# Attention with a mixture of experts: a new order of the first six slots, and nineteen fewer dummy matmuls

## The chip, the cores and the metric

The kernel runs on one core of a Trainium2 chip. The metric is the device time of one launch in microseconds (us). TensorE (PE) multiplies matrices, VectorE (DVE), ScalarE (ACT) and GpSimd (POOL) work on elements, and SyncE (SP) issues nearly all transfers.

## The reference

The first phase is causal attention over 8 batches of 8 heads, 576 positions of 64 features, with a bias that decays with the running sum of a learned scalar:

```python
scores = scale * np.matmul(q, k.transpose(0, 1, 3, 2))
s_pos = np.maximum(s, 0.0)
cum = np.cumsum(s_pos, axis=-1)
bias = -(cum[:, :, :, None] - cum[:, :, None, :])
scores = np.where(causal, -1000000000.0, scores + np.minimum(bias, 0.0))
scores = scores - np.max(scores, axis=-1, keepdims=True)
attn = np.exp(scores)
attn = attn / (np.sum(attn, axis=-1, keepdims=True) + 1e-09)
return np.matmul(attn, v).astype(np.float32)
```

The second phase takes its output as x (8 x 576 x 512). Each of 4 experts projects x to q, k and v of 64 features, does causal attention, and projects back by wo; each position sums the two experts that its gate logits rank highest, weighted by a softmax over the two.

## The kernel before

The work is cut into slots. A slot is a pair of heads of the first phase or a pair of experts of the second. For each slot there are: copies of the raw q and k to a high part in a short float format (L645 for q, L648 for k), subtractions that leave the low part (L688, L693), and a second copy of the raw q and k (L663, L666, L674, L679), so that a float32 product is made of a matmul with the low parts (L780, tiles `q_0` and `k_0` of the first kind) and one with the high parts, the bias rows and a row of minus the maxima (L786). Before the scores come approximate column maxima: bfloat16 matmuls (L714, tiles `mx`), a reduction on DVE (L728, `mcol`), a transpose (L749, `mt`), a copy on ACT (L753, `mr`), and a transfer of that row into the operand q (L758). Then ACT takes the exponential (L809), POOL masks and sums (L827 to L879), TensorE multiplies by v (L947) and ACT copies that out (L961, `pv`). Sums go by L895 or L997, a reciprocal (L1028), a row to DRAM and back (`rr`, `rb`, L1034 and L1039), and DVE scales (L1064). ACT and DVE then split x into a high part (L1068, `xh`) and a low part (L1072, `xl`), and TensorE projects (L1182, `pq`).

At the start the scalars s are loaded twice: for the first two slots in short pieces (`f_t`, L457), and for all (`s_t`, L492), scaled (L495), summed along rows (L496), completed by a matmul over the parts (L500), and split in three (L503 to L510); the result is written to DRAM (L1511, `cum`), from where later slots read their bias rows.

The order is by hand. Each instruction stands on its engine in the order in which the program calls the steps, and the steps are called as the table STEPS lists them: "n:x" is step x of slot n. In it m and M are the matmuls and the reduction of a bank of maxima, mt, mA and mq the transpose, copy and transfer of the row, s and E a bank of scores and its exponential, a the first matmuls of a bank of scores whose second part comes later, d masks and sums, e0 the last sum on POOL, b0 and B0 early sums of the rows on TensorE and their copy, h the high copies, l the low parts, lq and lk the second copies, hc the bias rows, p and P projections and their copies, ld, lv and w loads of heads, of v and of weights, cu to cx of slot -2 the running sums, cu of slot -1 the transfer of them to DRAM. A step named for slot n may belong to a slot ahead: what stands under slot -2 prepares slot 0. z is a dummy, a matmul of 128 columns (L1442) whose result nobody reads: five at the start and 48 in the table. Each is two passes on TensorE. Engines wait for each other by semaphores that follow from the operands; on each engine a later instruction never overtakes one that waits.

Of the kernel before, what the change touches and what calls it, by code (L numbers as in the profile page):

```python
# [13 lines left out]
OP = mybir.AluOpType  # L14
# [16 lines left out]
FIRST_IDLE, IDLE = 5, 48  # L31
# [49 lines left out]
def heads(t, at, c0, c1):  # L81
# [1482 lines left out]
```

## Time and profile before

| what | value |
|---|---|
| median of 3 runs | 636.24 us (635.65 to 637.52) |
| profiled execution | 635.62 us, its span 633.9 us |
| TensorE (PE) busy | 627.3 us, 99% of the span |
| VectorE (DVE) busy | 511.1 us, 81% |
| ScalarE (ACT) busy | 446.9 us, 70% |
| GpSimd (POOL) busy | 420.7 us, 66% |

The span runs from the first to the last instruction that the profiler recorded; the execution's time is 1.7 us longer. Busy time of TensorE holds the dummies too. Matmuls are pipelined, so a group's busy time is shorter than the sum of its durations.

### The profile page before, as it was taken

To read this page: it belongs to the slowest core of one execution; us is meant where nothing else is said; L and a number is where in the kernel's file an instruction comes from. 1 tells how busy PE (TensorE), PEld (TensorE's weight loads), DVE (VectorE), ACT (ScalarE), POOL (GpSimd) and SP (SyncE) were. 2 spreads that over 40 slices of the span, in tenths; PEclk is the share of its full clock that TensorE was granted. 3 is DMA by queue.
4 is the path that set the end of the run, shared out by engine and by line. 5 is a ranking of instruction groups with operands and counts; after the bars stand their busy time and mean duration, and the time that the engine had idled before them with its cause. 6 is when DMAs were issued, how large, how long until landed. Compare 5 with 4: busy or idle time off the path is not lost.

```text
span 633.9 us, 16442 instructions
## 1 busy us (share of the span) xinstructions
PE 627.3 (99%) x5912; PEld 533.8 (84%) x5912; DVE 511.1 (81%) x1447; ACT 446.9 (70%) x976; POOL 420.7 (66%) x527
## 2 busy tenths in 40 slices
PE   9999999999999999999999999999999999999997
PEld 7888988888888888788887898788888889788875
DVE  7989887976988978886889778798887978763784
ACT  8897678856786676775767766785676775576364
POOL 5665697768864976587667766588576676828030
PEclk9999999999999999999999999999999999999999
DMA  5555723553665267455725464672563543432404
GB/s 155 168 167 141 224 65 95 155 115 96 191 164 137 65 157 195 129 148 126 197 77 150 114 136 131 165 211 57 147 193 91 139 143 82 119 101 56 111 2 149
DMA packets 61966, 83.45 MB, mean 132 GB/s; under 512 B 27439, under 2 KB 36871, under 8 KB 61885
## 3 DMA queue, kind: packets, MB, share of 16 engines
q1 hardware_dynamic: 61741, 82.27, 48.0%
q8 instruction: 47, 0.77, 0.5%
q14 instruction: 34, 0.28, 0.1%
q10 hardware_dynamic: 144, 0.13, 0.1%
HBM read 44.60 MB, written 10.16 MB: 86 GB/s over the span
## 4 chain that ended last, share of the span: by engine, by line
PE 93%; ACT 3%; DVE 2%; DMA 1%; issue 0%; SPq 0%; ACTq 0%; DVEq 0%
PE pvp L947 20%; PE pq L1182 16%; PE s L780 12%; PE s L786 12%; PE mx L714 10%; PE pw L1182 7%; PE po L1182 7%; PE sm L997 4%; PE po L1151 1%; PE mt L749 1%; PE idle L1442 1%; DMA rb<-rr 1%; PE pw L1237 1%; PE pw L1242 1%; ACT k L648 1%; DVE unread L728 1%
## 5 line engine op out<-in xcount | busy, mean ns | idle before, releaser
L809 ACT ACTIVATE p<-s 128x512 f32<-128x512 f32 x288 | 159.1, 588 | 39.7 <-PE s L786 32.8
L728 DVE CUSTOM_DVE_ANT_0 unread<-mx,mask 128x256 uint8<-128x256 f32 (+6 forms) x384 | 142.2, 418 | 31.8 <-PE mx L714 30.5
L780 PE MATMUL s<-q,k 128*128 128x288 f32 (+5 forms) x672 | 166.9, 285 | 0.2 <-ACT p L809 0.2
L786 PE MATMUL s<-q,k 68*128 68x288 f32 (+5 forms) x672 | 159.9, 279 | 0.0
L827 POOL TENSOR_SCALAR_AFFINE_SELECT p<-p 128x256 f32<-128x256 f32 (+2 forms) x183 | 110.6, 606 | 71.7 <-ACT p L809 69.6
L780 PEld LDWEIGHTS s<-q,k 128*128 128x128 f32 (+1 forms) x672 | 122.3, 183 | 7.2 <-issue 2.2
L874 POOL TENSOR_TENSOR r<-r,p 128x640 f32<-128x640 f32 x84 | 120.4, 1433 | 6.8
L786 PEld LDWEIGHTS s<-q,k 68*128 68x128 f32 (+1 forms) x672 | 121.5, 182 | 1.1 <-DMA q<-mr 0.4
L688 DVE TENSOR_TENSOR q<-raw,q 64x576 fp32r<-64x576 f32 (+1 forms) x86 | 83.0, 974 | 21.6 <-ACT q L645 7.9
L947 PE MATMUL pvp<-p,v 128*64 128x64 f32 (+6 forms) x1024 | 99.6, 334 | 0.3 <-DVE mcol L728 0.3
L947 PEld LDWEIGHTS pvp<-p,v 128*64 128x64 f32 x1024 | 68.3, 136 | 23.7 <-ACT p L809 0.9
L693 DVE TENSOR_TENSOR k<-raw,k 64x576 fp32r<-64x576 f32 (+1 forms) x86 | 83.1, 976 | 5.3 <-DMA k<-k 3.3
L714 PE MATMUL mx<-k,q 67*64 67x320 bf16 (+7 forms) x960 | 81.6, 293 | 0.8 <-DVE mcol L728 0.6
L1182 PE MATMUL pq<-xh,wqkh 128*128 128x288 f32 x256 | 76.4, 299 | 0.0
L1182 PE MATMUL pq<-xl,wqkh 128*128 128x288 f32 x256 | 75.5, 295 | 0.0
L1182 PE MATMUL pq<-xh,wqkl 128*128 128x288 f32 x256 | 75.4, 295 | 0.0
L868 POOL TENSOR_TENSOR r<-p 128x128 f32<-128x128 f32 x37 | 22.3, 602 | 72.3 <-ACT p L809 72.3
L648 ACT ACTIVATE k<-raw 64x576 fp32r<-64x576 f32 x96 | 64.9, 680 | 3.1 <-DMA raw<-in_qk_dram 0.8
L714 PEld LDWEIGHTS <-q 67*64 67x64 bf16 x960 | 47.4, 109 | 22.2 <-issue 6.1
L645 ACT ACTIVATE q<-raw 64x576 fp32r<-64x576 f32 x96 | 64.9, 681 | 1.5 <-PE s L786 0.4
L961 ACT ACTIVATE pv<-pvp 128x256 f32<-128x256 f32 (+1 forms) x92 | 36.2, 402 | 36.5 <-PE pvp L947 35.7
L1200 ACT ACTIVATE raw<-pq 128x288 f32<-128x288 f32 x64 | 25.4, 404 | 35.2 <-PE pq L1182 35.2
(174 smaller groups left out, 1245.4 us busy)
## 6 DMA issues: line engine op xcount, KB each, us to landing
raw<-in_qk_dram SPq DMA_DIRECT2D x30, 576.0 KB
rb<-rr SPq DMA_DIRECT2D x92, 144.0 KB
q<-q SPq DMA_DIRECT2D x45, 288.0 KB
k<-k SPq DMA_DIRECT2D x39, 288.0 KB
v<-in_vm_dram SPq DMA_DIRECT2D x32, 256.0 KB
out_dram<-o SPq DMA_DIRECT2D x31, 256.0 KB
q<-mr SPq DMA_DIRECT2D x96, 2.2 KB
raw<-in_qk_dram SPq DMA_DIRECT2D x4, 288.0 KB
```

Source lines behind the costliest of these rows:

```text
L648: nc.scalar.activation(k2[0:64, j], get_raw(n, j)[64:128], AF.Copy)
L688: eng.tensor_tensor(a[64:128, j], get_raw(n, j)[0:64], q2[0:64, j].bitcast(F32), op=OP.subtract)
L693: eng.tensor_tensor(c[0:64, j], get_raw(n, j)[64:128], c[64:128, j].bitcast(F32), op=OP.subtract)
L714: nc.tensor.matmul(t[64 * j : 64 * j + 64, c0 : c0 + k1 - k0], q2[0:RC, 64 * qt : 64 * qt + 64], k2[0:RC, k0:k1], start=True, stop=True,)
L728: nc.vector.tensor_tensor_reduce(t[:, 0:w] if len(MBANKS[bi]) == 1 else unread[:, c0 and 448 : (c0 and 448) + w], t[:, c0 : c0 + w], mask[ ...
L780: nc.tensor.matmul(t[0:nk, c0 : c0 + q1 - q0], K1[r1(n)][:, j, k0 : k0 + nk], Q1[r1(n)][:, j, q0:q1], start=True, stop=False,)
L786: nc.tensor.matmul(t[0:nk, c0 : c0 + q1 - q0], K2[r2(n)][0 : RM + 1, j, k0 : k0 + nk], Q2[r2(n)][0 : RM + 1, j, q0:q1], start=False, stop= ...
L809: nc.scalar.activation(chunk_of(ci, 0, 512)[:, x % 2], tl[x], AF.Exp, scale=0.125)
L827: nc.gpsimd.affine_select(out=a, in_=a, pattern=[[0, a.shape[1]], [1, w]], compare_op=OP.is_ge, fill=0.0, base=0, channel_multiplier=-1,)
L874: add(r[:, :, q0:S], r[:, :, q0:S], chunk_of(2, c, c + S - q0), op=OP.add)
L947: nc.tensor.matmul(cur[h][64 * j : 64 * j + 64, q0 - PVC[h] : q1 - PVC[h]], vsl(j, kt), heads(ptile[n], at, c, c + q1 - q0)[:, j], start=f ...
L1182: nc.tensor.matmul(t[0:nk, 0:w], l, r, start=(x == 0), stop=(x == len(terms) - 1))
```

## The change

Nineteen dummies go: two ahead of the first complete score, and the seventeen that stood later, in the steps of slots 0 to 4. The scaling of the running sums moves from DVE to ACT, their last subtraction from DVE to POOL, the load of s behind the two loads of the first q and k, the transfer of the sums to DRAM behind the loads of v, and the second copy of slot 0's q on ACT is divided, the second head's part behind the copy of the maxima. Some 25 steps of slots 1 to 6 stand at other places in the table: high copies of slots 4 to 6, masks and sums of slots 1 to 4, maxima of slots 2 to 6, the early sums of slot 1, a bank of scores of slots 5 and 6, one load of heads, one of weights. Behind slot 6 the order is the same.

```diff
-FIRST_IDLE, IDLE = 5, 48
+FIRST_IDLE, IDLE = 5, 29
...
-    "-2:hc -2:cu -2:ld -2:h1 -2:h0 -2:z0 -2:z1 -2:z2 -2:z3 -2:z4 -2:cv -2:h3 -2:h2 -2:cw -2:cx 0:lc "
+    "0:lc -2:hc -2:cu -2:ld -2:h1 -2:h0 -2:z0 -2:z1 -2:z2 -2:z3 -2:z4 -2:cv -2:h3 -2:h2 -2:cw -2:cx "
...
-            nc.vector.tensor_scalar(rt, st, 0.0, 8.0, op0=OP.max, op1=OP.mult)
+            nc.scalar.activation(rt, st, AF.Relu, scale=8.0)
             nc.vector.tensor_tensor_scan(rt, rt, rt, 0.0, op0=OP.add, op1=OP.max)
...
         def last():
-            nc.vector.tensor_tensor(c3[:, 2], ct, c3[:, 1], op=OP.subtract)
+            nc.gpsimd.tensor_tensor(c3[:, 2], ct, c3[:, 1], op=OP.subtract)
...
             if not n:
-                for j in range(2):
-                    nc.scalar.activation(a[0:64, j], get_raw(n, j)[0:64], AF.Copy)
+                nc.scalar.activation(a[0:64, 0], get_raw(n, 0)[0:64], AF.Copy)
...
+        if not n:
+            items["lr"] = lambda: nc.scalar.activation(a[0:64, 1], get_raw(n, 1)[0:64], AF.Copy)
...
     first[0]()
+    call(load(0))
     rest[0]()
-    call(load(0))
     fill(0)
```

Line numbers in the changed kernel are one to three lower than before. The first place is the start of SP and of ACT; `f_t` and `s_t` are the loads of s, `raw` the loads of q and k. SP before:

```order
L457 DMA f_t<-in_s_dram 32x2x36
L492 DMA s_t<-in_s_dram 128x288
L589 DMA raw_137<-in_qk_dram 128x576 x2
L354 DMA k_0_71<-q_0_68 1x16x72
L626 DMA k_0_71<-p_75 3x32x36
L589 DMA raw_154<-in_qk_dram 128x576 x2
```

SP now:

```order
L455 DMA f_t<-in_s_dram 32x2x36
L587 DMA raw_136<-in_qk_dram 128x576 x2
L490 DMA s_t<-in_s_dram 128x288
L352 DMA k_0_71<-q_0_68 1x16x72
L624 DMA k_0_71<-p_75 3x32x36
L587 DMA raw_159<-in_qk_dram 128x576 x2
```

The load of s went behind both loads of q and k. ACT from its second instruction on, before:

```order
L367 ACTIVATE q_0_68<-p_75 32x1152
L371 ACTIVATE k_0_71<-p_75 32x1152
L648 ACTIVATE k_0_71<-raw_137 64x576
L645 ACTIVATE q_0_68<-raw_137 64x576
L648 ACTIVATE k_0_71<-raw_137 64x576
L645 ACTIVATE q_0_68<-raw_137 64x576
```

ACT now:

```order
L365 ACTIVATE q_0_68<-p_75 32x1152
L369 ACTIVATE k_0_71<-p_75 32x1152
L493 ACTIVATE s_r<-s_t 128x288
L646 ACTIVATE k_0_71<-raw_136 64x576
L643 ACTIVATE q_0_68<-raw_136 64x576
L646 ACTIVATE k_0_71<-raw_136 64x576
L643 ACTIVATE q_0_68<-raw_136 64x576
```

The scaling, which needs `s_t`, stands ahead of the first copy of k. The second place is the first scores on TensorE, before:

```order
L1442 MATMUL idle<-p_75 64x128 x3
L780 MATMUL s_4_313<-q_0_64,k_0_66 128x320
L780 MATMUL s_2_315<-q_0_64,k_0_66 128x256
L780 MATMUL s_0_317<-q_0_64,k_0_66 128x320
L1442 MATMUL idle<-p_75 64x128 x3
L786 MATMUL s_4_313<-q_0_68,k_0_71 128x320
```

TensorE there now:

```order
L1441 MATMUL idle<-p_75 64x128 x4
L779 MATMUL s_4_313<-q_0_64,k_0_66 128x320
L779 MATMUL s_2_315<-q_0_64,k_0_66 128x256
L779 MATMUL s_0_317<-q_0_64,k_0_66 128x320
L1441 MATMUL idle<-p_75 64x128
L785 MATMUL s_4_313<-q_0_68,k_0_71 128x320
```

Of the three dummies ahead of the first matmul that reads the row of maxima one is left there, and one stands ahead of the scores. The row's own transfer on SP, the same place, before:

```order
L629 DMA k_2_73<-p_75 1x4x288 x3
L1511 DMA cum<-p_75 384x1x288
L758 DMA q_0_68<-mr_271 1x9x64 x2
L591 DMA raw_275<-in_qk_dram 128x2x576
L601 DMA v_113<-in_vm_dram 128x2x256
```

And now:

```order
L627 DMA k_2_73<-p_75 1x4x288 x3
L757 DMA q_0_68<-mr_268 1x9x64 x2
L589 DMA raw_273<-in_qk_dram 128x2x576
L599 DMA v_113<-in_vm_dram 128x2x256
L600 DMA v_113<-in_vt_dram 64x2x64
L1510 DMA cum<-p_75 384x1x288
```

The sums (`cum`) went from ahead of the row (`mr`) to behind the loads of q, k and v. The third place is DVE ahead of the first projections, in the steps of slot 5, before:

```order
L1064 TENSOR_TENSOR pv_1021<-pv_1021,rb_1_1048 128x576
L1072 TENSOR_TENSOR xl<-pv_842,xh 128x576
L728 ISA mx_3_1126,mcol_1137<-mx_3_1126,mask 128x512
L728 ISA mcol_1137 128x1
L1072 TENSOR_TENSOR xl<-pv_1021,xh 128x576
```

DVE there now:

```order
L1063 TENSOR_TENSOR pv_1001<-pv_1001,rb_1_1029 128x576
L1071 TENSOR_TENSOR xl<-pv_828,xh 128x576
L1071 TENSOR_TENSOR xl<-pv_1001,xh 128x576
L727 ISA mx_3_1112,mcol_1132<-mx_3_1112,mask 128x512
L727 ISA mcol_1132 128x1
```

The reduction of a bank of maxima (`mx_3`) and the last low half of x (`xl`) changed places.

## Rows read from the trace of the kernel before

**Rows 1.** The page, part 1: busy us, share of the span, instructions.

```profile
PE 627.3 (99%) x5912; PEld 533.8 (84%) x5912; DVE 511.1 (81%) x1447; ACT 446.9 (70%) x976; POOL 420.7 (66%) x527
```

**Rows 2.** Busy us by stage; columns named in its first line.

```profile
core 0: us, PE busy (x) PEld busy (x) DVE busy (x) ACT busy (x) POOL busy (x), PEclk, DMA share, GB/s
18.40:47.90 29.50, 28.66 (x313) 24.45 (x314) 26.25 (x77) 28.52 (x59) 20.48 (x25) 1.00 0.52 161
47.90:61.00 13.10, 12.80 (x159) 11.24 (x156) 11.85 (x28) 9.44 (x19) 6.69 (x8) 1.00 0.60 162
61.00:70.70 9.70, 9.70 (x103) 8.07 (x103) 9.43 (x25) 7.84 (x18) 8.18 (x16) 1.00 0.63 169
70.70:620.00 549.30, 549.05 (x5161) 467.61 (x5159) 443.36 (x1248) 379.68 (x843) 374.63 (x456) 1.00 0.48 127
```

**Rows 3.** TensorE's waits: us in total, times, longest.

```profile
PE mx L714 <- DVE mcol L728: 0.6, 1, 0.6
```

**Rows 4.** Timeline, SP's issues: start us, us, operation, idle before.

```profile
1.27 0.41 SPq L492 DMA_DIRECT2D s_t<-in_s_dram  x1
1.72 0.91 SPq L589 DMA_DIRECT2D raw<-in_qk_dram  x2
...
12.92 0.64 SPq L1511 DMA_DIRECT2D cum<-p  x1
...
13.65 1.55 SPq L758 DMA_DIRECT2D q<-mr  x2
```

**Rows 5.** Transfers: issues and KB of each.

```profile
q<-mr SPq DMA_DIRECT2D x96, 2.2 KB
raw<-in_qk_dram SPq DMA_DIRECT2D x4, 288.0 KB
...
cum<-p SPq DMA_DIRECT2D x1, 432.0 KB
...
s_t<-in_s_dram SPq DMA_DIRECT2D x1, 144.0 KB
```

**Rows 6.** By half microseconds, columns as in rows 2.

```profile
5.00:5.50 0.50, 0.50 (x4) 0.50 (x3) 0.47 (x2) 0.28 (x1) 0.00 (x0) 1.00 0.13 44
```

**Rows 7.** Timeline, the first copies and the first maxima.

```profile
3.27 1.16 ACT L371 ACTIVATE k<-p 32x1152 fp32r<-32x1152 f32 x1
...
4.89 0.31 DVE L495 TENSOR_SCALAR s_r<-s_t 128x288 f32<-128x288 f32 x1
5.22 0.68 ACT L648 ACTIVATE k<-raw 64x576 fp32r<-64x576 f32 x1 [0.79 <-DMA raw<-in_qk_dram]
...
8.08 1.47 PE L714 MATMUL mx<-k,q 67*64 67x448 bf16 x20
```

**Rows 8.** The page, part 5: count, busy us, mean ns, idle before.

```profile
L780 PE MATMUL s<-q,k 128*128 128x288 f32 (+5 forms) x672 | 166.9, 285 | 0.2 <-ACT p L809 0.2
...
L1200 ACT ACTIVATE raw<-pq 128x288 f32<-128x288 f32 x64 | 25.4, 404 | 35.2 <-PE pq L1182 35.2
```

**Rows 9.** Timeline, the first scores.

```profile
15.43 0.88 PE L1442 MATMUL idle<-p 128*64 128x128 f32 x6
...
16.23 0.19 PEld L786 LDWEIGHTS s<-q,k 68*128 68x128 f32 x1 [0.17 <-DMA q<-mr]
...
16.96 0.60 ACT L809 ACTIVATE p<-s 128x512 f32<-128x512 f32 x1 [0.96 <-PE s L786]
```

**Rows 10.** Timeline, dummies: passes in the last column.

```profile
3.57 2.40 PE L1442 MATMUL idle<-p 128*64 128x128 f32 x10
...
6.49 1.77 PE L1442 MATMUL idle<-p 128*64 128x128 f32 x14
...
50.36 0.83 PE L1442 MATMUL idle<-p 128*64 128x128 f32 x6
```

**Rows 11.** Timeline, POOL ahead of the early sums.

```profile
49.97 0.40 POOL L848 TENSOR_SCALAR r<-p 128x256 f32<-128x256 f32 x1
```

**Rows 12.** Timeline, ACT and DVE ahead of the first projections.

```profile
68.81 0.67 ACT L1068 ACTIVATE xh<-pv 128x576 fp32r<-128x576 f32 x1
...
69.29 0.69 DVE L728 CUSTOM_DVE_ANT_0 mx<-mx,mask 128x512 f32<-128x512 f32 x1
...
69.90 0.75 DVE L1072 TENSOR_TENSOR xl<-pv,xh 128x576 fp32r<-128x576 f32 x1
```

426 rows, old and new, of the table STEPS are left out of this document.

## The prediction

> **What bounds the kernel now.** I read the share of busy time first. TensorE is busy 627.3 of 633.9 us [rows 1], so on the whole it is the bound; but a share is an average, and the change touches only the first 70 us. So the busy times by stage come next [rows 2]. From 70.7 us on TensorE works 549.05 of 549.30 us: whatever the first slots gain or lose is handed through to the end unchanged. In 18.4 to 47.9 us two engines are full at once: TensorE 28.66 us of 29.50, but with dummies in it, and ACT 28.52 us, of which no instruction is a dummy. There ACT is the real limit: its idle time is 0.98 us in all. From 47.9 to 61 us TensorE has 12.80 of 13.10 and DVE 11.85; from 61 to 70.7 us DVE has 9.43 of 9.70. The list of TensorE's waits then shows how little the dummies leave open: the longest inside these slots is 0.6 us for the column maxima of DVE [rows 3]. Before 18.4 us no stage view helps, since there the work is one chain; I follow it in the timeline: the loads of the scalars s and of q and k [rows 4], ACT's copies of k and q, the first maxima on TensorE [rows 7], the first scores [rows 9].
>
> All sums are on the profiled execution, 635.62 us with its span of 633.9. The median of the runs is 636.24, so 0.62 is added at the end.
>
> **Part 1: the first copies.** The load of s (144 KB) stood ahead of the two loads of q and k (288 KB each) [rows 4, 5]; the change puts it behind them, and puts a new Relu on ACT, which needs it, ahead of the first copy of k. ACT is free at 3.27 + 1.16 = 4.43 us, and its first copy starts at 5.22, released by the load of q and k; the s that DVE reads was there by 4.89 at the latest [rows 7]. The bytes of all these loads have come in by about 5.2 us: in 5.0 to 5.5 us the transfers take 0.13 of the engines and 44 GB/s [rows 6]. With s last, its bytes are the last of the same total, so it is usable not before some 5.2 us, and if it is released as late behind its bytes as the first q and k were (they are the first 441 of 729 KB, and were released at 5.22) up to 1 us later. I take 5.9. The Relu costs about 0.40 us (ACT's copy of the same 128x288 elements takes 404 ns [rows 8]), so the first copy starts at 6.3 and not at 5.22: **+1.1**. Bounds: s is there when ACT is free, then 4.43 + 0.40 = 4.83, **-0.4**; s at 6.2, then **+1.4**. Everything up to the first maxima hangs on the copies: TensorE starts them at 8.08 us, when ACT's fourth copy is done [rows 7]; TensorE's dummies ahead of them only fill the time, so one fewer there is worth nothing. Two steps leave DVE: the scaling (0.31 us [rows 7]), and the last part of the sums, which goes to POOL, whose next step waits for ACT's copies anyway. DVE's scan starts 1.1 us later like the copies, with one step fewer between it and the first reduction, so DVE is there when its maxima are, and I cost both at nothing.
>
> The Trainium skill has a rule that speaks against this edit: DMA: Bandwidth & Descriptors, section Queues, rings and completion order, says that each DMA engine takes up the descriptors of a ring in their order. By it the 144 KB of s start only when 576 KB are taken up. By the opposite view, each transfer on its own, s would be there at ACT's first free moment and the sum would be 1.5 us lower. No row of before has s behind a large load.
>
> **Part 2: the row of maxima and the first scores.** The 2.2 KB row of minus the maxima is issued right behind the 432 KB of the running sums (12.92, then 13.65 us) [rows 4, 5]. The score matmul that reads it starts at 16.24, and its weight load waited 0.17 us for it; three dummies stand ahead [rows 9]. The change sends the sums behind the loads of v and leaves one of these three dummies, and moves one of them in front of the scores. Neither alone would help, both together do: the matmul can start one dummy (two passes of 0.12, below) after 15.43, at 15.67. **-0.55**; between 0, if the row is itself as slow without the sums ahead of it, and -0.6. The copy of q's second head is put behind the maxima's copy on ACT; POOL's subtractions, which release the first score at 14.8, need the hi part and not that copy: nothing. ACT's first exponential, which waited 0.96 us for the score [rows 9], moves with it.
>
> **Part 3: the seventeen later dummies.** Each is two passes; a pass takes 0.12 us ((1.77 - 0.83) / (14 - 6) [rows 10]), so 34 passes are 4.0 us of TensorE. Twenty of them lie before 47.9 us, where ACT is full: TensorE then waits where it now idles along. Only ACT's own 0.98 us of idle time can go, and part of that is releases, not TensorE's lateness: **-0.3**, between 0 and -1.0. Of the other fourteen, six stand at 50.36 in front of the early sums, which POOL's step released at 49.97 + 0.40 = 50.37 [rows 11]: with nothing there the sums could start 0.7 us sooner; but behind them DVE's chain of normalization (reciprocal, row to DRAM and back, scaling) is not on TensorE's time. I take 0 and keep -0.7 as the bound.
>
> **Part 4: the moved steps.** Two end last in their stage. On DVE the bank reduction at 69.29 (0.69 us) goes behind the low half of x that now starts at 69.90 [rows 12]; that half needs ACT's high half, done at 68.81 + 0.67 = 69.48. So it starts 0.4 us sooner: **-0.4**, between 0 and -0.6. TensorE's projections need it just there. And a score step of slot 5 (four matmuls) goes ahead of the first projection and a maximum behind it, so that TensorE has more to do until x is ready: four matmuls at 166.9 / 672 = 0.25 us of busy time [rows 8], taken at half of it for their overlap, are worth 0.5 us where it would wait: **-0.25**, between 0 and -0.5. The other twenty-odd moves (copies of slots 2 to 6 later, POOL's masks and sums earlier or later, maxima behind other banks, one load of slot 8) shift work by a step or two on engines that stay as busy as they are [rows 2]; behind them stand exponentials that are in their old order. I cost them at nothing together, 0.5 us either way; their transfers are the same number in nearly the same order.
>
> Sum: +1.1 - 0.55 - 0.3 - 0.4 - 0.25 = -0.4. 635.62 - 0.4 + 0.62 = **635.8 us**. What can be told from no change here is 0.3%, 1.9 us: 634.33 to 638.15.
>
> **Rivals.**
> TensorE is the bound, and the dummies count in full. For it speak 99% of busy time and a wait list that is nearly empty [rows 1, 3]; against it ACT's 28.52 of 29.50 us without a dummy. If true, the order moves exist to let TensorE run ahead, and 4.0 us go while the start keeps its +0.55: -3.45, but DVE's 9.43 of 9.70 us at the end of the stretch would give back some 0.3: 635.62 - 3.15 + 0.62 = 633.1 us. Chance 0.22.
>
> s arrives in time. Then part 1 is -0.4 and not +1.1, and the sum is -1.9: 634.3 us, on the border. For it: DVE started on s at 4.89, before any q and k were used. Against: 576 KB stand ahead of it. Chance 0.13.
>
> TensorE falls to half speed. Rows first: the ten passes at 3.57 take 0.24 us each, the fourteen at 6.49 some 0.126 [rows 10]; the granted clock stands at 1.00 in all stretches listed [rows 2, 6], so I take the level from the passes: the early ones fit 1.2 GHz, the later ones 2.4. Before the rise TensorE had run dummies almost without a pause. Now the matmul of the running sums, at whose place the rise falls, waits for the Relu about 1 us longer, and the gaps of the slots have no dummies. If the slow level lasts through the twelve dummies ahead of the maxima, they run 12 x 0.114 = 1.4 us longer, and the first bank of maxima some 0.45; a second fall in the slots, where twelve to twenty passes filled the gaps, would add an equal amount of waiting, about 1.6. Together +3.4 on the sum: 635.62 - 0.4 + 3.4 + 0.62 = 639.2 us. It decides from 2.3 us lost, that is twenty passes' worth at the slow level. Against it: ACT's bound hides part of such a loss, and TensorE stays over nine tenths busy in the slots. Chance 0.14.
> The Trainium skill, TensorE: Matmul & The Clock Gate, Part 1, calls the throttled state the default, which activity releases; that TensorE began slow agrees with it, 0.24 us a pass against 0.126, and no run here shows a fall inside the slots yet.
>
> **How the numbers follow.** The forecast has 0.51. Its own range: upwards half of each part's upper bound and half of the 0.5 for the other moves add to 1.1; downwards, the early s being a rival, the halves for parts 2 to 4 and the moves add to 1.2: with 0.2 for the spread of runs, 634.4 to 637.1. The rivals have 0.22, 0.13 and 0.14. Faster by over 0.3%: all of the first rival, half of the second, 0.03 from the forecast: 0.32. Slower: all of the third and 0.01 from the forecast: 0.15. Within: 0.53. The range that leaves out two in ten ends at the first rival's own time, so that half of it is below, and short of the third: 633.1 to 638.0.
>
> **What would show it.** ACT's first copy of k at about 6.3 us, waiting for the Relu and the Relu for s; if at 4.9, the second rival holds. The first maxima near 9.2. The first score matmul that reads the row about 0.6 us after the first score is done, and not 1.4. TensorE's busy time down by about 4.5 us while the span hardly moves, its wait list longer by some 3 us in 20 to 48 us with ACT as the releaser; ACT's idle time in that stretch still under 1 us. If TensorE's waits do not grow, the first rival is right. The dummies behind the running sums at 0.24 us a pass would show the third. I am wrong on part 4 if TensorE shows a wait for x at the first projections.

## The result, and the profile after

The changed kernel takes 642.76 us (median of 5 runs, 642.34 to 645.2) against 636.24 before: a ratio of 1.0113, 95% interval 1.0096 to 1.0129, or 6.5 us more. That is slower, outside the range of 633.1 to 638.0, and a forecast of 635.8 was wrong by 7. The profiled execution is the one of 642.76 us, with a span of 641.0. Of e12, below, only the times are used, since its profiled execution ran at a granted clock of 0.56 throughout (1009.8 us).

The page of the changed kernel, part 1 (compare [rows 1]):

```profile
PE 629.5 (98%) x5874; PEld 532.3 (83%) x5874; DVE 513.5 (80%) x1445; ACT 447.7 (70%) x977; POOL 423.1 (66%) x528
```

TensorE has 38 passes fewer and is busy 2.2 us longer. So the loss is not only waiting: some of its passes ran slower. Busy time by stage, cut at the same events as [rows 2] (columns there):

```profile
20.10:52.00 31.90, 29.03 (x291) 23.79 (x289) 25.95 (x75) 27.73 (x58) 21.19 (x24) 0.95 0.51 163
52.00:65.20 13.20, 12.54 (x147) 9.48 (x149) 11.89 (x28) 9.97 (x21) 6.66 (x9) 1.00 0.60 161
65.20:75.00 9.80, 9.80 (x105) 8.07 (x102) 8.79 (x26) 7.96 (x18) 9.13 (x17) 1.00 0.53 148
75.00:626.00 551.00, 550.23 (x5159) 467.72 (x5158) 447.73 (x1250) 380.54 (x843) 374.53 (x456) 1.00 0.48 127
```

The stages take 31.90, 13.20, 9.80 and 551.00 us, where they took 29.50, 13.10, 9.70 and 549.30. With 1.7 us ahead of them (20.10 against 18.40) and 1.1 behind (15.0 against 13.9) the sum is +7.1, the whole difference of the spans. Two things are to be seen at once: the loss lies in three places (the start, the first stage, and 1.7 + 1.1 us behind 75 us, where the order of the instructions is unchanged), and the granted clock of the first stage is 0.95.

To place it more finely I use one instruction of each slot: the transpose of the maxima on TensorE (`mt`). Number of slot and shift of its start against before, in the profiled executions:

| slot | 0 | 1 | 2 | 3 | 4 | 6 | 12 | 44 | end of span |
|---|---|---|---|---|---|---|---|---|---|
| changed kernel, us | +1.89 | +1.67 | +2.17 | +2.43 | +4.83 | +4.33 | +4.97 | +5.11 | +7.15 |

So: 1.9 at the start, 0.5 from slot 1 to 2, 2.4 from slot 3 to 4, 0.6 from slot 6 to 12, 2.0 behind slot 44. The last is only seen by somebody who compares the ends, too. The waits of TensorE from 20 to 76 us (columns as in [rows 3]):

```profile
PE mx L713 <- ACT k L646: 1.4, 1, 1.4
PE s L779 <- DVE k L692: 0.9, 2, 0.7
PE s L785 <- DMA q<-mr: 0.5, 1, 0.5
PE pvp L946 <- ACT p L808: 0.4, 1, 0.4
```

The 0.6 us of [rows 3] is gone, and new ones stand here. The timeline of the changed kernel shows the instructions of each place (columns: start, us, engine, line, operation, tiles, form, idle before and releaser):

```profile
5.45 0.44 ACT L493 ACTIVATE s_r<-s_t 128x288 f32<-128x288 f32 x1 [1.02 <-DMA s_t<-in_s_dram]
5.92 0.68 ACT L646 ACTIVATE k<-raw 64x576 fp32r<-64x576 f32 x1
...
6.83 0.56 PE L498 MATMUL cs<-s_r,p 128*128 128x1 f32 x2 [0.87 <-DVE s_r L494]
7.32 2.39 PE L1441 MATMUL idle<-p 128*64 128x128 f32 x10
9.29 0.58 PE L713 MATMUL mx<-k,q 67*64 67x448 bf16 x1
...
10.54 0.62 DVE L727 CUSTOM_DVE_ANT_0 unread<-mx,mask 128x448 uint8<-128x448 f32 x1 [1.48 <-PE mx L713]
...
16.94 0.68 PE L779 MATMUL s<-q,k 128*128 128x320 f32 x3
...
17.91 0.42 PE L785 MATMUL s<-q,k 68*128 68x320 f32 x1
...
18.91 0.62 SPq L1510 DMA_DIRECT2D cum<-p  x1
20.38 1.58 SPq L757 DMA_DIRECT2D q<-mr  x2
...
24.24 0.41 PE L785 MATMUL s<-q,k 68*128 68x320 f32 x1 [0.47 <-DMA q<-mr]
...
39.03 0.68 ACT L646 ACTIVATE k<-raw 64x576 fp32r<-64x576 f32 x1
39.77 0.34 PE L713 MATMUL mx<-k,q 67*64 67x384 bf16 x2 [1.37 <-ACT k L646]
```

**Start.** ACT waited 1.02 us for s, and its first copy of k starts at 5.92, not at 5.22 [rows 7]. Then TensorE's ten passes behind the running sums take 0.24 us each, where fourteen took 0.126 [rows 10], and DVE's first reduction comes at 10.54; before it was at 8.65. Of the kernel before, that reduction and the first scores (the first one, and the first that reads the row):

```profile
8.65 0.62 DVE L728 CUSTOM_DVE_ANT_0 unread<-mx,mask 128x448 uint8<-128x448 f32 x1
...
14.82 0.68 PE L780 MATMUL s<-q,k 128*128 128x320 f32 x3
...
16.24 0.42 PE L786 MATMUL s<-q,k 68*128 68x320 f32 x1
```

The trace's entries on the granted clock fit the passes: the first entry, at the full level of 2.4 GHz, begins at 10.05 us here and at 6.28 before. For the time ahead of it there is no entry, and a stretch counts such time as 1.00; so the 1.00 of [rows 6] says nothing of the first 6 us.

**Slot 1's row of maxima.** The transfer of the sums (`cum`, 432 KB) is issued at 18.91, and the row of slot 1 (`mr`, 2.2 KB) behind it at 20.38. The row is not on TensorE before 24.24. Slot 1's row of the kernel before, with no such transfer in front of it, had landed 1.90 us after its issue. In the chain of waits:

```profile
20.38 3.82 DMA q<-mr
```

**Slot 4's copy of k.** The first maxima of slot 4 wait 1.37 us for a copy that ACT begins at 39.03. Just behind it the granted clock (PEclk, the third number from the right) is 0.50, the lower level of 1.2 GHz:

```profile
38.00:39.00 1.00, 0.40 (x3) 0.11 (x1) 0.97 (x2) 1.00 (x3) 0.00 (x0) 1.00 1.04 309
...
41.00:42.00 1.00, 1.00 (x8) 0.87 (x6) 0.64 (x1) 0.64 (x1) 1.00 (x2) 0.50 0.56 178
42.00:43.00 1.00, 1.00 (x11) 0.93 (x9) 0.83 (x6) 0.00 (x0) 0.92 (x2) 0.50 0.88 188
43.00:44.00 1.00, 1.00 (x12) 0.86 (x9) 0.47 (x1) 0.83 (x3) 0.92 (x3) 0.50 0.95 361
```

**The end.** ACT, which copies the last results out, waits for a buffer until an earlier store has left it. The timeline, and the DMA queues in 630 to 637 us (packets, MB, share):

```profile
635.78 1.15 ACT L1157 ACTIVATE o<-po 128x512 f32<-128x512 f32 x3 [2.06 <-DMA out_dram<-o]
```

```profile
q1 hardware_dynamic: 698, 1.27, 48.2%
q8 instruction: 1, 0.02, 1.2%
```

The store was issued at 631.67. Fifteen of its 16 engines were done by 633.73, the last at 635.62; the two stores behind it have one such late engine each. In the same stretch, at 632.71, one packet of q8 passed, a queue that the page calls "instruction"; before, the last packet of q8 is 16.8 us ahead of the end. (A second queue of that name, q14, has a packet some 4 us ahead of the end in every profile.) The profile before has no such wait of ACT.

### The profile page after: what moved, and what is told of

It reads as the page before. It is cut to its first block, busy times and chain, and to the rows that moved or that the text cites. A ratio compares the mean times of both kernels' runs of the same rounds, so it can differ in the third digit from the quotient of the medians.

```text
span 641.0 us, 16364 instructions
## 1 busy us (share of the span) xinstructions
PE 629.5 (98%) x5874; PEld 532.3 (83%) x5874; DVE 513.5 (80%) x1445; ACT 447.7 (70%) x977; POOL 423.1 (66%) x528
## 4 chain that ended last, share of the span: by engine, by line
PE 89%; ACT 4%; DMA 3%; DVE 1%; POOL 1%; issue 1%; SPq 0%; ACTq 0%; DVEq 0%
PE pvp L946 19%; PE pq L1181 15%; PE s L779 12%; PE s L785 12%; PE mx L713 9%; PE pw L1181 7%; PE po L1181 7%; PE sm L996 3%; ACT p L808 1%; DMA raw<-in_qk_dram 1%; PE mt L748 1%; ACT k L646 1%; PE pw L1236 1%; DMA out_dram<-o 1%; PE pw L1241 1%; PE idle L1441 1%
## 5 line engine op out<-in xcount | busy, mean ns | idle before, releaser
L946 PE MATMUL pvp<-p,v 128*64 128x64 f32 (+6 forms) x1024 | 100.9, 337 | 0.7 <-ACT p L808 0.4
L713 PE MATMUL mx<-k,q 67*64 67x320 bf16 (+7 forms) x960 | 83.9, 295 | 1.8 <-ACT k L646 1.4
L1063 DVE TENSOR_TENSOR pv<-pv,rb 128x576 f32<-128x576 f32 x46 | 41.9, 915 | 10.7 <-DMA rb<-rr 9.3
```

What stands on the lines that cost most here:

```text
L713: nc.tensor.matmul(t[64 * j : 64 * j + 64, c0 : c0 + k1 - k0], q2[0:RC, 64 * qt : 64 * qt + 64], k2[0:RC, k0:k1], start=True, stop=True,)
L946: nc.tensor.matmul(cur[h][64 * j : 64 * j + 64, q0 - PVC[h] : q1 - PVC[h]], vsl(j, kt), heads(ptile[n], at, c, c + q1 - q0)[:, j], start=f ...
```

## The experiments

All ratios are against the kernel before, with their 95% interval; 0.001 is 0.64 us. In the diffs only words of the table that move are shown, of e2 only some of them.

**First: which half of the change?** e1 has the changed start with the old order and the later dummies; e2 the old start with the changed order and without the later dummies; e3 only leaves out the seventeen; e4 puts them back into the changed kernel.

e1, against the kernel before:

```diff
-FIRST_IDLE, IDLE = 5, 48
+FIRST_IDLE, IDLE = 5, 46
...
-    rest[0]()
     call(load(0))
+    rest[0]()
```

> The kernel before with the changed start alone: load of s behind q and k, Relu on ACT, last subtraction on POOL, divided copy of q, transfer of the sums behind v, two dummies fewer; the seventeen later dummies and the order of slots 1 to 6 as before. Theory A (the start and the rows of maxima behind the sums cost over 2 us, the rest comes from slots 2 to 4): about +2.2 us on before, first exponential at 18.6 us and the second slot's transpose +0.5 us later than the first one's shift; TensorE's dummies behind the running sums at 0.24 us a pass; no fall of the clock later. Rival B (nearly everything follows from the slow start, since later waits line up differently): +5 us or more. Rival C (the later dummies and moves carry all): +0.5 us or less.

e2, against the kernel before:

```diff
-FIRST_IDLE, IDLE = 5, 48
+FIRST_IDLE, IDLE = 5, 31
...
-1:ld 2:h1 2:M5
+1:ld 2:M5
...
-2:lk 2:h3 2:v3
+2:lk 2:v3
...
-2:s1 2:h2 2:s4 2:s0
+2:s1 2:s0
...
+1:d0 2:h2 2:s4 2:h3 2:E3
```

> The kernel before with the other half: its old start, but the seventeen later dummies gone and the steps of slots 1 to 6 moved as changed. Theory A: about +2.5 to +3.5 us, with a wait of TensorE of over 1 us for ACT's k copy of slot 4 near 36 us and a stretch of some 3 us of granted clock 0.5 behind it. Rival B: within 0.5 us of before. Rival C: about +6 us.

e3, against the kernel before, and e4, which puts the same words into the changed kernel:

```diff
-1:h3 -2:z31 1:v3 -2:z32 1:h0
+1:h3 1:v3 1:h0
```

> The kernel before with nothing but the seventeen later dummies taken out. If the dummies keep TensorE's clock up by themselves: +2 us or more, with a stretch of granted clock 0.5 between 30 and 50 us. If they only fill waits, and the moved steps cause the long wait: between -1.0 and +0.3 us and a granted clock of 1.00 throughout. If TensorE was the bound there: -3 us.

> The changed kernel with the seventeen later dummies back at their old places in the order. If the dummies keep the clock up: 2 to 3 us faster than the changed kernel (some 640 us), no stretch at half clock. If the moved steps cause the loss: within 0.7 us of the changed kernel, the wait for ACT's k copy near 39 us still there, partly filled, and the clock perhaps still at 1.00.

Measured: e1 1.0023 (0.9998 to 1.0049), e2 1.0024 (1.0007 to 1.0040), e3 1.0007 (0.9990 to 1.0025), e4 1.0081 (1.0049 to 1.0113). Each half costs about 1.5 us (e1's interval includes no loss at all), the two together 7.2: the parts do not add. And the dummies are worth some 2 us in the changed kernel (1.0113 to 1.0081, with intervals that overlap), 0.5 and perhaps nothing in the kernel before. So I repaired the changed kernel one part at a time.

**Second: single repairs of the changed kernel.** e5 puts two dummies into the pause ahead of the matmul of the running sums; e6 loads s first again; e7 puts the three high copies of slot 4 and one bank of scores back to their old places; e8 sends the sums behind slot 1's row.

```diff
--2:z4 -2:cv
+-2:z4 -2:z5 -2:z6 -2:cv
```

> The changed kernel with two more dummies ahead of the matmul of the running sums, where TensorE now pauses 0.87 us. If the pause is what keeps TensorE at half clock behind it: the ten to twelve passes behind the sums at 0.12 instead of 0.24 us, the first maxima at 8.8 us and the first reduction at 9.3 instead of 10.5, so 1.2 us off the start, and 641.5 us or less. Rival: the rise has nothing to do with the pause, and the passes stay at 0.24 us; then 0 to +0.3 us.

```diff
-    call(load(0))
     rest[0]()
+    call(load(0))
```

> The changed kernel with the load of s again ahead of the loads of q and k; the Relu stays on ACT. If ACT waits for s because it is queued behind the large loads: Relu at 4.5 to 4.9 instead of 5.45 us, the first copy of k at 5.2 to 5.4, the sums' matmul at 6.3 instead of 6.83 with a pause of 0.35, and 1.2 to 1.9 us off the start (about 641 us). If the transfer is as late anyway: no difference.

```diff
-1:ld 2:M5
+1:ld 2:h1 2:M5
...
-1:v1 2:h1 2:M4
+1:v1 2:M4
...
-2:lk 2:v3
+2:lk 2:h3 2:v3
...
-2:s1 2:s0
+2:s1 2:h2 2:s4 2:s0
...
-1:d0 2:h2 2:s4 2:h3 2:E3
+1:d0 2:E3
```

> The changed kernel with four steps of slot 4 back at their old places: the high copies of q and k (three of them) and one bank of slot 2's scores. If the wait of 1.37 us for ACT's k copy at 38.4 us and the fall of the clock behind it come from these moves: the wait gone, the clock at 1.00 throughout, the transposes of slots 4 and later 2 to 2.5 us earlier, about 640.5 us. Rival (ACT is late there whatever the order): the wait only moves, within 0.7 us of the changed kernel.

```diff
-0:lv -1:cu -1:m0
+0:lv -1:m0
...
-0:mq 1:lv
+0:mq -1:cu 1:lv
```

> The changed kernel with the 432 KB of the running sums one place later still, behind the second slot's row of maxima. If this transfer delays the small row (3.82 us from issue to landing now): the row lands within 2.5 us, TensorE's wait of 0.5 us for it goes and slot 2 comes 0.5 us earlier, about 642.2 us. Rival (the row is late because of the loads of q, k and v ahead of it): no difference. Bias rows of later slots read the sums back; if they become the later ones, +0.5 us instead.

Measured: e5 1.0074 (1.0056 to 1.0093), e6 1.0110 (1.0058 to 1.0163), e7 1.0075 (1.0060 to 1.0090), e8 1.0094 (1.0068 to 1.0120). e7 gains 2.4 us: its wait for the copy is gone, and slot 7 stands at +0.28. From slot 2 to 6 it gains 0.5 us where the changed kernel loses 2.2; but another 1.25 us between the two profiles lie at the start, which its edit does not touch. e5 gains as much by time, though in its profile the copy's wait is still 1.4 us. Its start is 1.2 us better than the changed kernel's, which e7 and e8 have without the extra dummies; and behind slot 44 it loses 0.1 us and not 2.0, for a reason that the fourth group shows. e6 is a miss: nothing gained, with runs from 639.4 to 647.7. The start itself is repaired (slot 0 stands at -0.30), but its profiled execution has a granted clock of 0.65 to 0.83 from 20 to 50 us, and the gain is buried. e8 shows that a wait can stand behind a wait. In its timeline:

```profile
7.06 1.55 PE L1452 MATMUL idle<-p 128*64 128x128 f32 x12
...
22.24 0.39 PE L790 MATMUL s<-q,k 128*128 128x320 f32 x1 [0.27 <-DVE k L703]
```

The row, with the sums behind it, lands 2.58 us after its issue and not 3.82, so the sums held it up by some 1.2. It no longer ends last, but the same scores now wait for DVE's low part of k. The first line matters later: 0.13 us a pass, though s came as late as in the changed kernel.

**Third: everything from the good side.** e9 is the changed start, with s first, the old order and all later dummies. e10 is the changed kernel with three parts undone together: s first, the dummies, the copies of slot 4. e11 moves only these copies (and their bank of scores) in the kernel before. e12 is e10 with s still late.

e9, against e1 (e10 has the same lines against e12):

```diff
-    call(load(0))
     rest[0]()
+    call(load(0))
```

> The changed start (Relu on ACT, last subtraction on POOL, divided copy of q, sums behind v, two dummies fewer) with the load of s back ahead of q and k, and behind it the old order with all later dummies. If the load of s is the fault in the start: first transpose of maxima 0.3 us before the old one, slot 2 within +0.2 us, no loss against before, 635.3 to 636.5 us where the same start with s behind was 1.5 us slower. If the sums' new place costs 0.5 us by the second slot's row, slot 2 comes 0.1 us late and the whole is even. Rival (Relu on ACT is the fault): still +1 us.

> The changed kernel with three things undone: load of s ahead, the seventeen dummies back, four steps of slot 4 at their old places. The other moves stay. If these three are the loss: within 0.7 us of before, clock at 1.00 throughout, no wait of TensorE over 0.8 us. Rival (the remaining moves cost too, or the loss is spread): +1.5 us or more.

e11, against the kernel before (e12 has these lines the other way round, against e4):

```diff
-1:ld 2:h1 2:M5
+1:ld 2:M5
...
-1:v1 2:M4
+1:v1 2:h1 2:M4
...
-2:lk 2:h3 2:v3
+2:lk 2:v3
...
-2:s1 2:h2 2:s4 2:s0
+2:s1 2:s0
...
+1:d0 2:h2 2:s4 2:h3 2:E3
```

> The kernel before with the four steps of slot 4 alone moved to their new places; dummies and start as before. If the move of the copies by itself makes TensorE wait for ACT: a wait of about 1 us for the k copy near 35 us and +0.5 to +1.5 us. If it does so only together with the late start: no wait, within 0.4 us of before.

> The changed kernel with the seventeen dummies and the four steps of slot 4 back, the start as changed. Against the run with s ahead as well it tells what the start costs: if 1.0 to 1.9 us, about 637.5 us here. Against the run with the dummies alone back (640.96) it tells the copies: if they cost 2 to 2.5 us with a late start, 638.5 us here. Rival (these costs don't add): 640 us or more.

Measured: e9 0.9989 (0.9976 to 1.0002), e10 0.9996 (0.9983 to 1.0009), e11 1.0026 (1.0011 to 1.0041), e12 1.0017 (1.0004 to 1.0030). Three faults undone, and the kernel is even with before. The remaining moves, more than twenty, cost no more than can be measured (0.8 us either way). e11 shows the copies' wait alone, in a kernel in which nothing else is changed, in its waits from 30 to 45 us and on ACT's timeline:

```profile
PE mx L725 <- ACT k L659: 1.4, 1, 1.4
```

```profile
36.53 0.60 ACT L820 ACTIVATE p<-s 128x512 f32<-128x512 f32 x1 [0.23 <-ACT p L820]
37.03 0.25 ACT L764 ACTIVATE mr<-mt 9x128 fp32r<-9x128 f32 x1
37.18 0.67 ACT L656 ACTIVATE q<-raw 64x576 fp32r<-64x576 f32 x1
37.88 0.68 ACT L659 ACTIVATE k<-raw 64x576 fp32r<-64x576 f32 x1
```

The copy of k stands fourth here, behind an exponential, the row of maxima and the copy of q: it starts 1.35 us after that exponential does, and TensorE has nothing else to do. Its price is less sure than its wait. The profiled span of e11 is 3.2 us longer than before, and 1.8 of that stand at the start, where no instruction is changed and the clock's first entry begins at 10.29 us; from slot 2 to slot 12 the copies lose 0.7. So the 1.65 us of the times may hold some of the start, and 0.7 to 1.65 is what can be said. In e9 the start:

```profile
4.46 0.44 ACT L506 ACTIVATE s_r<-s_t 128x288 f32<-128x288 f32 x1
5.00 0.68 ACT L659 ACTIVATE k<-raw 64x576 fp32r<-64x576 f32 x1
```

With s first, Relu starts 0.99 us and the copy 0.92 us sooner than in the changed kernel. Against e1 that is worth 0.0034, or 2.2 us; against e12, e10 gains 0.0021, or 1.3.

**Fourth: the dummies.** Each of three kernels again without them: e13 is e10, e14 is e9, e15 is e1. e16 asks whether e9 gains if the sums go behind slot 1's row. e17 and e18 are e14 and e9 with the last results in buffers of their own, so that ACT's last copies cannot wait for a store.

```diff
-1:h3 -2:z29 1:v3 -2:z30 1:h0
+1:h3 1:v3 1:h0
```

> The repaired kernel (load of s ahead, four steps of slot 4 at their old places, the remaining moves as changed) without the seventeen later dummies. If the dummies are free once the two faults are gone: 635.5 to 636.7 us, as with them (635.98). If TensorE's clock needs them wherever the order is the changed one: 638.5 us or more, with stretches of granted clock 0.5.

> The changed start with the load of s ahead, the old order behind it, without the seventeen dummies. If the dummies only matter with the moves: within 0.7 us of before. If the new start (its late row for the second slot) needs them: 637.5 us or more, and a fall of the clock between 20 and 60 us in some stretch.

> The changed start as it is, with s late, the old order behind it, without the seventeen dummies. If costs add: late s 1.5 and dummies 0.5, so 638 us. If the late start makes the missing dummies dear: 639.5 to 641 us.

```diff
-0:lv -1:cu -1:m0
+0:lv -1:m0
...
-0:mq 1:lv
+0:mq -1:cu 1:lv
```

> The changed start with s ahead, old order and dummies, and the transfer of the running sums one place later, behind the second slot's row of maxima. If that transfer is what took back the start's 0.43 us: the row lands 2.5 us after its issue and not 3.9, slot 2 and all later ones 0.4 us ahead of before, 635.4 us. Rival (DVE's low part of k is next in line and takes it back): even with before.

```diff
-sb.tile([P, 2, S], F32, tag="raw", name=f"o{b}_{tt}", bufs=3)
+sb.tile([P, 2, S], F32, tag="r" if b == B - 1 else "raw", name=f"o{b}_{tt}", bufs=3)
```

> The new start with s ahead, old order, no later dummies (as e14, 638.88 us), and the last batch's output tiles in other buffers, so that ACT's last copies don't wait for the stores of the batch before. If the late store explains what the dummies are worth beyond the slots: ACT's wait of 1.8 us at 628.6 gone, 1.0 to 1.8 us faster than e14, 637.0 to 637.9 us; a packet of code still lies among the last stores. Rival (the end is late for another reason): as e14.

> The same buffers in the kernel with the dummies (as e9, 635.69 us), where no code is loaded among the last stores: within 0.4 us of e9, since ACT waits for no store there. Rival: a general gain of over 0.8 us, which would say that the buffers and not the code load are the point.

Measured: e13 1.0049 (1.0027 to 1.0070), e14 1.0034 (1.0015 to 1.0052), e15 1.0086 (1.0057 to 1.0114), e16 1.0000 (0.9987 to 1.0014), e17 1.0015 (1.0000 to 1.0030), e18 1.0001 (0.9988 to 1.0013). With the changed start, leaving out 4.0 us of work that nobody reads costs 3.4 us (e10 to e13), 2.9 (e9 to e14), 4.0 (e1 to e15) and 3.7 (e12 to e7), after the 2.0 of e4; each of these differences is sure to some 1.5 us, those with e1 and e4 to some 2.4. e16 gains nothing, as e8 had shown, though its row lands in 2.63 us. The last copies on ACT in e14, and then in e17:

```profile
630.42 1.15 ACT L1168 ACTIVATE o<-po 128x512 f32<-128x512 f32 x3 [1.77 <-DMA out_dram<-o]
```

```profile
629.53 1.04 ACT L1168 ACTIVATE o<-po 128x512 f32<-128x512 f32 x2 [0.76 <-PE po L1161]
```

With buffers of its own ACT waits for TensorE, and 1.2 us come back by the ratios (1.0034 to 1.0015); in e9, which has no such wait, the same edit gives nothing (e18). The two intervals overlap, so the times alone do not settle it. The profiles do: in e17 one engine of the same store is still late (fifteen done by 628.75, the last at 630.51), ACT no longer waits for it, and the stretch behind slot 44 is 1.0 us shorter than in e14.

It is not a rule of every kernel without the dummies. A packet of q8 falls among the last stores in all eleven profiles without them and in none of the eight with them; but ACT waits for the store in six (the changed kernel, e6, e7, e13, e14, e15), not in e2, e3, e5 and e8, and e17 cannot. (The wait of e6, 2.20 us, is put down to TensorE by its row; but its copy starts 0.15 us behind the store's last engine, as in the others.) The traces tell the two kinds apart. There are 47 packets of q8 in every profile. Counted in TensorE's records (matmuls, weight loads and those of its sequencer), the last one starts when 11,944 to 11,964 of them have begun, in all nineteen profiles. With 46 or 48 dummies in the table 118 to 127 records are left then, with 31 (e2, e3, e5) 55, with 29 only 30 to 41. So each pass that goes moves the packet further into the tail. With 31 dummies it starts 0.8 us ahead of the store's issue, in e8 1.95 us behind it, and the store's last engine ends within 0.3 us of the fifteenth. In the other seven it starts 0.96 to 1.24 us behind the issue, and the last engine ends 1.5 to 2.0 us after the fifteenth. (In e8 it is 1.11 us behind the next store, and there the last engine is 1.7 us late.) That the packet holds this engine up is the reading; no run moves the packet alone.

No kernel here beats the one before by more than can be told; e9, 0.7 us by its ratio, is the nearest.

## Why the prediction was wrong

**What failed.** The first step that failed is the sentence that what the first slots gain or lose "is handed through to the end unchanged". Of the 7.15 us between the profiled spans 2.8 arise behind slot 6, where no instruction is moved. By this sentence part 3 could only gain: it priced the dummies by ACT's idle time in the slots, at -0.3, and they cost some 3. The second is the nothing for the other moves, of which three cost 0.7 to 1.65 us. The third is the start: part 1 had the late s, and the slow passes behind it stood in a rival of 0.14. So the mechanism was wrong, and not only the sum.

**Part 1 (+1.1 said, +0.7 measured at the first copy).** The direction and the reason held: the Relu starts at 5.45, and at 4.46 with s first, so s landed behind the loads of q and k. The Trainium skill, DMA: Bandwidth & Descriptors, section Queues, rings and completion order, which has each DMA engine consume descriptors in ring order, agrees with these two starts. The second rival (s in time) is out for the kernel as changed; where it said -0.4, e9 shows -0.22 with s first (5.00 against 5.22). The sum left out the other 1.2 us of the start, the slow passes, which the third rival had at 1.4. They are not always there: the first reduction is at 10.1 to 10.9 in four of seven profiles with s late (changed, e1, e4, e15) and at 9.3 or earlier in e5, e7 and e8; with s first it is late in one of twelve. That one is e11, whose start is that of before:

```profile
6.14 0.56 PE L511 MATMUL cs<-s_r,p 128*128 128x1 f32 x2 [0.17 <-DVE s_r L507]
6.63 2.82 PE L1453 MATMUL idle<-p 128*64 128x128 f32 x12
```

A pause of 0.17 us, and 0.235 us a pass; e8 had a pause of 1.43 and fast passes. So the longer pause is not shown to be the cause. The same instructions at the start can do either, and how often they do each is not known. Nor is late s shown to be: e5, e7 and e8 were run on one chip, e1, e4 and e15 on two others.

**Part 2 (-0.55 said; -0.45 measured, then lost).** The score that reads slot 0's row starts 0.97 us after the first score (17.91 - 16.94), where it took 1.42 (16.24 - 14.82), and that row lands 1.84 us after its issue, where it took 2.39; the step was right. But I followed the large transfer only to where it left, not to where it arrived. It now stands in front of slot 1's row, which takes 3.82 us from its issue in the changed kernel and 3.92 in e9, and slot 2 loses 0.5. In e9 slot 1 is 0.43 ahead of before and slot 2 is 0.14 behind: the gain is given back one slot later. Part 2 has no term for what stands behind the new place, and where part 4 says that the transfers are "the same number in nearly the same order" it does not count this one.

**Part 3 (-0.3 said, +2 to +4 measured with the changed start).** This is the largest failure. I argued only about how much of 4.0 us could be saved, and my bounds were 0 and -1.0. That a removal could cost time stood only in the third rival, at 1.6 us. For the slots it touches the forecast was near: from slot 0 to slot 6 the removal gains 0.55 us in e14 (against e9) and 0.1 in e13 (against e10). What the runs show behind them: from slot 6 to 44 a loss of 0.9 and 1.1 us, so that 0.2 and 0.6 us are lost at slot 44; and at the end of the span another 1.7 to 1.9, where a store is late on one engine and ACT waits 1.8 to 2.0 us for its buffer. e17 takes 1.2 us of that back. In some executions the granted clock falls inside the slots as well. Of e3, the two stretches in which it does:

```profile
50.00:55.00 5.00, 3.01 (x46) 2.36 (x48) 3.41 (x5) 1.74 (x4) 3.08 (x3) 0.82 0.77 190
55.00:60.00 5.00, 5.00 (x45) 4.64 (x43) 3.39 (x5) 4.07 (x10) 0.53 (x1) 0.84 0.51 168
```

In the first of them TensorE is busy 3.01 of 5 us. e3's longest wait, for POOL's `r`, lies in the place of the six dummies of [rows 10]:

```profile
PE es L904 <- POOL r L857: 2.2, 1, 2.2
```

That was a cost I had put as a chance of -0.7. POOL's step in front of it takes 1.60 us there, where it takes 0.40 in [rows 11]; e14, e15 and e17, the others with the old order and no dummies, show the same step and the same wait. So the third rival was right in what it feared, clock and empty gaps, and e15 has a fall too (0.66 in 55 to 60 us); but the clock stays at 1.00 in e4 behind the same wait of 1.4 us that the changed kernel has, and the rival's 639.2 left out the end and the copies. The old start is not what spares e2 and e3 the last wait: e5 has the new one, and like them 31 dummies, and is spared too; it is the count of passes that places the packet. What stays open: the rest of why leaving out the dummies costs 0.5 us at most with the old start (e3, and e2 against e11) and 2 to 4 with the new, above all the 0.9 to 1.1 us from slot 6 to 44, and why the clock falls in some executions and not in others.

**Part 4 (-0.65 said, nothing measured; the other moves at 0, +0.7 to +1.65 measured).** I priced "the other twenty-odd moves" as a heap, because the engines stay as busy as they are. Nearly all of them are worth nothing, as e10 shows. But three of them put ACT's copies for slot 4 behind other work, one copy ends last, and TensorE waits 1.4 us for it in e11, which moves nothing else: 1.65 us by its times, 0.7 in the slots of its profile; e7 gets 2.4 back. The two gains I did count are not seen, and [rows 2] could have told: TensorE is busy 9.70 of 9.70 us there, so there was no wait to shorten. In the changed kernel DVE does reduce behind the low halves of x:

```profile
72.97 1.81 DVE L1071 TENSOR_TENSOR xl<-pv,xh 128x576 fp32r<-128x576 f32 x2
...
74.69 0.69 DVE L727 CUSTOM_DVE_ANT_0 mx<-mx,mask 128x512 f32<-128x512 f32 x1
```

but TensorE had other matmuls to do until then, as before: e10, with both moves, starts its first projection at 69.51, e9 without them at 69.33, the kernel before at 69.32.

**The bound.** I said ACT was the real limit of the first stage, and that its idle time would stay under 1 us. It is 31.90 - 27.73 = 4.17 us now. The first rival, TensorE as the bound, is out as well: 4 us of its work went, and the time grew. Between these two full engines a single chain (a copy, a row, a store) ended last each time. That is what neither of my shares could show.

**The sum as measured.** Late s 1.3 to 2.2 us, copies 0.7 to 1.65, dummies 2.9 to 3.4: 4.9 to 7.2, against 6.5 by the medians and 7.2 by the ratio. These three prices are from kernels in which the rest was sound, and each is sure to 1 or 2 us only. That the three together are the loss rests on e10. From the first four runs, the sum would have been 3.

## What to carry to other kernels

When a large transfer is moved on a queue, name the small ones that it now stands in front of, and do the same for a copy on an engine that works in order: who waits for it, and what does that engine have to do meanwhile. Matmuls that nobody reads are not free to remove, even where the engine looks full with them: time the removal by itself, in the new surroundings, and look at the end of the span too: what is gained early need not arrive there. Parts of a change that spoil each other are priced by undoing them from the sound side, all but one.

## What the runs showed of the hardware

- A 2.2 KB row issued 1.5 us behind a transfer of 432 KB took 3.82 us (3.92 in e9); with that transfer behind it, 2.58 (e8) and 2.63 (e16); in the kernel before, 1.90.
- A 256 KB store can be late by one engine alone: fifteen done by 633.73, the sixteenth at 635.62. I had taken the store's end for the end of its bytes. In the seven profiles in which this store has a late engine, and in no other, a 16 KB packet of q8 ("instruction") had started 0.96 to 1.24 us after its issue.
- The packets of q8 go by TensorE's instructions: 47 in every profile, 255 to 256 of TensorE's records from one to the next in the mean, so that fewer passes put the last one later in the program.
- The rise to the full clock comes at different times after the same instructions: the clock's first entry at 6.28 us before, at 10.29 in e11 (0.126 and 0.235 us a pass). It is worth 1.8 us (first reduction at 8.65 and 10.46). In fourteen of nineteen profiles it comes at 4.2 to 6.3 us, in the changed kernel, e1, e11 and e15 at 10.0 to 10.7, in e4, after a fall, at 11.1.
